# A spectral-mixing kernel: one channel staged through SBUF rows, and a new order of the opening

## Chip, cores and metric

One NeuronCore of one Trainium2 chip. The metric is the device time of one execution in microseconds (us). The four jobs of experiments ran on three different chips, so a time is compared with the kernel before of the same job.

Names in the profile: PE is TensorE and PEld its weight loads, ACT is ScalarE, DVE VectorE, POOL GpSimd, SP (or SPq) SyncE, which here only issues DMAs. The granted clock is the share of full speed that TensorE was allowed. A DMA lands when its completion has been counted in full. A packet is one recorded piece of a DMA.

## The reference

```python
def _attn_ref(x):                       # x: (8, 3008, 256) float32
    X = np.fft.fft(x, axis=1)           # DFT over the sequence
    X = np.fft.fft(X, axis=2)           # DFT over the channels
    return X.real.astype(np.float32)

def _moe_ref(x, w_in, w_out):           # (24064, 256), (256, 2048), (2048, 256)
    h = x @ w_in
    g = h * np.cos(h)
    return (g @ w_out).astype(np.float32)
```

The kernel folds the channel DFT into w_in (tiles Wc, Ws) and uses the symmetry of real input: rows are folded first, then a DFT over the sequence gives Rr (its real part, even in the channel), Ir (its imaginary part, odd in the channel) and, for channel 128 alone, one row per batch that is spread to 128 partitions in Rb. The main loop is 376 steps; a step makes two blocks of h in a PSUM bank H, cos(h) on ScalarE, products on VectorE and GpSimd, and the second matrix product on TensorE. Below, "even R" and "odd I" are the real part at the even and the imaginary part at the odd frequencies of the sequence; each is two groups of matmuls (halves).

## The kernel before

Channel 128 of batches 1 to 7 needs one float out of every row of x, 1 KB apart. Four loads (rows from the start, from the end, downwards and upwards from the middle) collect it in a DRAM scratch; four more DMAs then bring it to 128 partitions in runs of six.

```python
    def load_ext(j):
        first, step = ((0, 1), (SEQ, -1), (HALF, -1), (HALF, 1))[j]

        def copy(s0, s1, row, step):
            nc.sync.dma_start(
                out=xe_dr[j, :, s0:s1],                      # DRAM, 4 bytes each
                in_=bass.AP(tensor=xt, offset=x.offset + row * ND + 128,
                    ap=[[SEQ * ND, NB], [step * ND, s1 - s0], [1, 1]]),
            )
        ...
    def get_ext():
        xs = state["xs"] = spool.tile([128, 4, NB, 6], FP, tag="xs", ...)
        for j in range(4):
            nc.sync.dma_start(out=xs[:, j], in_=xe_dr[j].rearrange("b (p m) -> p b m", m=6))
```

The end of the weight fold sends one row of Ws through DRAM to a column layout. wex is what every first activation of a step (`ext`) needs:

```python
        nc.gpsimd.dma_start(out=wx_dr, in_=Ws[127:128, :])
        ...
            nc.gpsimd.dma_start(out=wex, in_=wx_dr.rearrange("o (f p) -> p (o f)", p=128))
```

The opening, and the places of the loads in the program order (T is one step):

```python
    fold_weights()
    EO, ops = fold_x(L_first, nc.vector, 1)
    fold_now("x1 c0 e0 o0 c3 e3 o3 c2 e2 E2 o2 O2 c1 e1 E0 EO0")   # x1 is a copy on ScalarE
    d = Dft(0, 0, 0, EO[0])          # even R
    ...
    d2 = Dft(1, 0, 0, EO[2])         # even I
    ...
    xb = fold_first(L_first)         # channel 128 of batch 0, broadcast
    d3 = Dft(0, 0, 0, xb, ring=Rb, first=True)
    ...
    at_dft(1, 2, 0, 0, 1, lambda: EO[1])      # odd R in steps 1 to 3
    at_dft(5, 2, 0, 1, 1, lambda: EO[3])      # odd I in steps 5 to 7
    for j in range(4):
        at((2 * j - 1) * T + 0.2, lambda j=j: load_ext(j))
    at(8 * T, get_ext)
    at(11 * T + 1.35, fold_ext)               # GpSimd
    at(11 * T + 4.75, dft_ext)                # TensorE: the DFT of step 11
```

The DFT of step 11 stands in TensorE's program ahead of all later steps. While it waited, TensorE ran nothing (no instruction in the stretch from 120 to 140 us below).

## Time and profile before

| | |
|---|---|
| time, median of 3 | 2106.68 us |
| span of the profiled execution | 2099.5 us |
| PE busy | 1980.4 us, 94% |
| PE busy from 200 to 2000 us | 99 to 100% in nearly all stretches of 100 us |
| longest wait of PE | 82.2 us, before the DFT of step 11 |
| start of step 0 | 48.05 us |
| DFT of step 11 | 199.82 us |

First the list of waits of PE before: who waited for whom, us in total, times, longest us.

```profile
PE H L228 <- POOL xe L237: 82.2, 1, 82.2
PE H L228 <- ACT H L240: 8.2, 6, 5.8
PE H L228 <- DMA w<-in_moe_w_in_dram: 7.6, 2, 6.7
PE pA L228 <- DVE e L287: 4.0, 1, 4.0
...
PE H L228 <- PE H L228: 0.7, 1, 0.7
```

One wait dominates. GpSimd (POOL) itself is only the messenger; its own list of waits names the DMA behind it.

```profile
POOL xs L237 <- DMA xs<-xe_dr: 83.0, 1, 83.0
```

The chain of work that ended last, before, in order of time (start us, us, what), follows this back. L431 is `load_ext`, L451 `get_ext`, SPq the SyncE queue that issues them.

```profile
24.08 5.47 DMA wx<-Ws
29.84 17.09 DMA wex<-wx
48.05 2.09 PE H L228 x4
...
73.41 40.54 SPq L431
114.00 35.50 SPq L431
149.61 33.12 SPq L451
...
196.33 2.63 DMA xs<-xe_dr
199.82 4.97 PE H L228 x26
```

Each issue takes 33 to 41 us, about the time of one load; I read this as a queue that is full of the load before it. The chain also shows the second hole: wex takes 17.09 us, and step 0 begins at 48.05 us. The table of stretches (us; busy us of each engine with instruction counts; then granted PE clock, DMA share, GB/s) shows PE idle and the clock at half, while the DMA engines are 98% busy at 1 GB/s: very many tiny transfers.

```profile
core 0: us, PE busy (x) PEld busy (x) DVE busy (x) ACT busy (x) POOL busy (x), PEclk, DMA share, GB/s
40.00:60.00 20.00, 12.03 (x27) 7.06 (x26) 6.25 (x11) 8.63 (x16) 9.24 (x19) 0.66 1.06 61
120.00:140.00 20.00, 0.00 (x0) 0.00 (x0) 0.00 (x0) 0.00 (x0) 0.00 (x0) 0.53 0.98 1
200.00:220.00 20.00, 19.14 (x93) 14.05 (x90) 9.48 (x17) 12.47 (x24) 14.05 (x21) 0.92 0.14 22
```

### The profile page before, as it was taken

What the parts mean: (1) busy time and instruction counts of PE and PEld (TensorE: products, weight loads), DVE (VectorE), ACT (ScalarE), POOL (GpSimd) and SP (SyncE); (2) the same over time, 40 slices, a digit from 0 to 9 for tenths busy, and PEclk for the clock granted to TensorE, in tenths of its full rate; (3) what the DMA queues carried; (4) which work ended last, traced back from release to release, by engine and by line L of the source; (5) the groups of instructions that cost most, each with busy time, mean ns of one, the idle gap of its engine ahead of it and who ended that gap; (6) DMA issues with size and microseconds to landing.
All of it is one profiled execution on the core that took longest, in us unless ns stands there. A gap on an engine that the chain in (4) does not pass through costs nothing.

```text
span 2099.5 us, 27859 instructions
## 1 busy us (share of the span) xinstructions
PE 1980.4 (94%) x8838; PEld 1651.8 (79%) x8838; DVE 1402.6 (67%) x2276; ACT 1433.3 (68%) x2730; POOL 1337.9 (64%) x1842
## 2 busy tenths in 40 slices
PE   6921999999999999999999999999999999999997
PEld 3711888888888888888888888888888888887886
DVE  3520766777767776677767776677766776667776
ACT  1610776777667776677767776677767776677775
POOL 3611775677648775678747786577756776555664
PEclk9865999999999999999999999999999999999999
DMA  9886120012100111002010121012110000100101
GB/s 248 48 1 13 42 63 11 15 28 71 19 16 13 47 45 25 11 17 66 23 21 17 37 56 18 11 19 55 41 20 15 18 15 17 18 11 11 21 11 20
DMA packets 252075, 66.80 MB, mean 32 GB/s; under 512 B 242162, under 2 KB 245002, under 8 KB 251418
## 3 DMA queue, kind: packets, MB, share of 16 engines
q1 hardware_dynamic: 249514, 52.43, 17.6%
q0 software_dynamic: 2416, 12.61, 2.2%
q8 instruction: 70, 1.15, 0.2%
q14 instruction: 75, 0.61, 0.1%
HBM read 40.26 MB, written 24.80 MB: 31 GB/s over the span
## 4 chain that ended last, share of the span: by engine, by line
PE 86%; SPq 6%; DMA 2%; DVE 2%; POOL 1%; ACT 1%; issue 1%; another core or an unknown queue 0%; DVEq 0%; POOLq 0%; ACTq 0%
PE H L228 36%; PE pB L228 14%; PE pC L228 14%; PE pD L228 14%; PE pA L228 7%; SPq L431 4%; SPq L451 2%; POOL G L237 1%; DMA wex<-wx 1%; DVE G L594 1%; DMA w<-in_moe_w_in_dram 1%; ACT G L240 1%; DVE G L234 0%; DMA wx<-Ws 0%
## 5 line engine op out<-in xcount | busy, mean ns | idle before, releaser
L237 POOL TENSOR_TENSOR G<-G 128x256 f32<-128x256 f32 x1504 | 1080.9, 729 | 629.0 <-DVE G L594 532.0
L594 DVE SCALAR_TENSOR_TENSOR G<-H,G 128x512 f32<-128x512 f32 x376 | 257.4, 685 | 402.1 <-ACT G L240 402.0
L240 ACT ACTIVATE E<-H 128x512 f32<-128x512 f32 x376 | 224.4, 597 | 351.9 <-PE H L228 348.5
L234 DVE TENSOR_TENSOR G<-H,G 128x512 f32<-128x512 f32 x376 | 260.0, 691 | 223.8 <-ACT G L240 220.7
L228 PE MATMUL H<-Rr,Wc 128*128 128x256 f32 x1504 | 395.8, 386 | 8.2 <-ACT H L240 8.2
L228 PE MATMUL H<-Ir,Ws 127*128 127x256 f32 x1504 | 389.5, 381 | 1.5 <-ACT E L240 1.5
L228 PE MATMUL pC<-G,WT 128*128 128x256 f32 x1504 | 387.0, 379 | 0.6 <-DVE u L234 0.4
L240 ACT ACTIVATE G<-H 128x512 int32<-128x512 f32 x376 | 224.6, 597 | 237.7 <-DVE G L234 237.7
L240 ACT ACTIVATE H<-Rb,wex 128x256 f32<-128x256 f32 x752 | 360.4, 479 | 25.4 <-DMA wex<-wx 6.1
L228 PEld LDWEIGHTS H<-Rr,Wc 128*128 128x128 f32 x1504 | 281.2, 191 | 53.7 <-ACT H L240 10.9
L228 PEld LDWEIGHTS H<-Ir,Ws 127*128 127x128 f32 x1504 | 283.6, 190 | 46.2 <-ACT E L240 7.5
L228 PEld LDWEIGHTS pC<-G,WT 128*128 128x128 f32 x1504 | 284.3, 189 | 42.8 <-PE H L228 2.5
L240 ACT ACTIVATE G<-G,halfpi 128x512 f32<-128x512 f32 x376 | 269.2, 716 | 0.3 <-DVE G L234 0.3
L234 DVE TENSOR_TENSOR G<-E,H 128x512 f32<-128x512 f32 x376 | 255.6, 680 | 10.8 <-issue 9.6
L234 DVE TENSOR_TENSOR M<-G,M 128x512 f32<-128x512 f32 x376 | 257.7, 685 | 0.0
L594 DVE SCALAR_TENSOR_TENSOR G<-G,M 128x512 f32<-128x512 f32 x376 | 254.4, 677 | 0.3 <-ACT M L240 0.3
L240 ACT ACTIVATE M<-M,halfpi 128x512 f32<-128x512 f32 x376 | 246.2, 655 | 0.1
L228 PE MATMUL pB<-G,WT 128*128 128x256 f32 x752 | 227.5, 384 | 2.6 <-POOL G L237 2.6
L240 ACT ACTIVATE M<-G 128x512 int32<-128x512 f32 x376 | 224.1, 596 | 0.0
L228 PE MATMUL pA<-G,w 128*128 128x256 f32 x752 | 223.7, 379 | 0.0
L228 PE MATMUL pB<-G,w 128*128 128x256 f32 x752 | 223.7, 379 | 0.0
L228 PE MATMUL pD<-G,w 128*128 128x256 f32 x752 | 223.7, 379 | 0.0
(100 smaller groups left out, 1761.6 us busy)
## 6 DMA issues: line engine op xcount, KB each, us to landing
out_dram<-ot SPq DMA_DIRECT2D x504, 32.0 KB
xl<-in_x_dram SPq DMA_DIRECT2D x16, 768.0 KB
MC<-dft_mats SPq DMA_DIRECT2D x4, 1131.0 KB
out_dram<-ot SPq DMA_DIRECT2D x256, 2.0 KB
Rb<-r SPq DMA_DIRECT2D x10, 376.0 KB
w<-in_moe_w_in_dram SPq DMA_DIRECT2D x4, 512.0 KB
w<-in_moe_w_out_dram SPq DMA_DIRECT2D x1, 2048.0 KB
out_dram<-ot SPq DMA_DIRECT2D x64, 28.0 KB
```

The lines of the kernel that those rows point to most:

```text
L228: nc.tensor.matmul(out_, lhsT=lhsT, rhs=rhs, start=start, stop=stop, skip_group_check=True)
L234: pin(nc.vector.tensor_tensor(out=o, in0=a, in1=b, op=op))
L237: pin(nc.gpsimd.tensor_tensor(out=o, in0=a, in1=b, op=op))
L240: pin(nc.scalar.activation(out=o, in_=i, func=func, **kw))
L431: nc.sync.dma_start(out=xe_dr[j, :, s0:s1], in_=bass.AP(tensor=xt, offset=x.offset + row * ND + 128, ap=[[SEQ * ND, NB], [step * ND, s1 - ...
L451: nc.sync.dma_start(out=xs[:, j], in_=xe_dr[j].rearrange("b (p m) -> p b m", m=6))
L594: nc.vector.scalar_tensor_tensor(out=o, in0=h, scalar=TWO_PI, in1=c, op0=ALU.mult, op1=ALU.mult)
```

## The change

The intent: take channel 128 off the critical path by loading it into SBUF rows first and storing whole rows to DRAM; issue it earlier; and start step 0 earlier with a new order of the opening. Cut to its core:

```diff
+    halfpi2 = cpool.tile([128, 1], FP, tag="halfpi2")
+    nc.vector.memset(halfpi2, 0.0)
...
         ops["x1", 0] = lambda: pin(
-            (nc.scalar.copy if eng is nc.vector else eng.tensor_copy)(
+            eng.tensor_copy(
...
     def load_ext(j):
-        first, step = ((0, 1), (SEQ, -1), (HALF, -1), (HALF, 1))[j]
+        if j == 0:
+            state["x1"] = spool.tile([128, HALF + 1], FP, tag="rx", bufs=1, name="x1")
+        t = state["x1"][j * NB : (j + 1) * NB]
         def copy(s0, s1, row, step):
             nc.sync.dma_start(
-                out=xe_dr[j, :, s0:s1],
+                out=t[:, s0:s1],
...
+        nc.sync.dma_start(out=xe_dr[j], in_=t[:, 0:768])
...
+    for _ in range(8):                                   # warm PE
+        mm(bank("M"), zero[:, 0:128], zero[:, 0:1].to_broadcast([1, 512]), True)
+    sin(halfpi2)                                         # load the sine table early
     fold_weights()
...
-    fold_now("x1 c0 e0 o0 c3 e3 o3 c2 e2 E2 o2 O2 c1 e1 E0 EO0")
...
+    fold_now("z1 z3 c0 e0 o0 c3 e3 c2 e2 E2 x1 c1 e1 E0 EO0")
+    dft_now(R_even, 1, "pA")
+    dft_now(R_even, 0, "pB")
+    xb = fold_first(L_first)
+    fold_now("o3 o2 O2 o1")
...                                                      # then broadcast channel, even I
-    at_dft(1, 2, 0, 0, 1, lambda: EO[1])
-    at_dft(5, 2, 0, 1, 1, lambda: EO[3])
+    for t, fn in (
...
+        (3.1, lambda: dft_now(R_odd, 1, "pB")),          # odd R in step 0
+        (3.2, lambda: dft_now(R_odd, 0, "pC")),
...
+        (T + 3.1, lambda: dft_now(I_odd, 1, "pD")),      # odd I in step 1
+        (T + 3.2, lambda: dft_now(I_odd, 0, "pA")),
...
     for j in range(4):
-        at((2 * j - 1) * T + 0.2, lambda j=j: load_ext(j))
+        at(-T, lambda j=j: load_ext(j))
...
-        l0 = max(0, s0 - 8)
+        l0 = s0 - (8 if b > 1 else 1.5)                  # loads of batch 1 earlier
```

## The prediction

> **What bounds it now.** From 200 us to the end PE is busy 99% (stretches of 100 us); a step takes 4.75 us (chain of waits) and the change touches nothing there. In the first 200 us PE has three holes. (1) Its longest wait in the list of waits: 82.2 us, 117.6 to 199.8 us, before the channel-128 DFT of step 11; POOL, ahead of it, waits 83.0 us for the DMA of xs from xe_dr. (2) Step 0 starts at 48.05 us because ACT waits until 47.0 us for wex, a DMA issued at 29.84 us, 17.1 us to landing. (3) Steps 0 and 1 have PE gaps of about 1 us, granted clock 0.66 (40 to 60 us), and a 1.28 us table load before the sine at 55.32 us.
>
> **Cause of (1).** The four loads of channel 128 move 6144 elements of 4 bytes each, DRAM to DRAM. The packet records from 95 to 180 us show 170 to 190 elements per us, 16 packets in flight, about 80 ns each: 34 us a load. Most took 9 ns, some about 400 ns, and a load begins with 1000 to 1300 elements in its first 2 us. I read that as fast reads that choke on 4-byte DRAM writes. Two loads into SBUF support this: wex is 2048 elements of 4 bytes, 512 bytes apart, and its packets ran from 32.3 to 33.5 us; xs (24-byte runs) reached 1300 runs per us.
>
> **Cause of (2).** The wex packets were done by 33.5 us, the semaphore landed at 47. The Trainium skill ("DMA: Bandwidth & Descriptors", Queues, rings and completion order) says a completion lands only after every earlier write of that DMA engine, across queues; here the writes of load 0 of channel 128. The trace agrees (13 us between).
>
> **What the change does.** Loads go to 8 SBUF rows, then 3072-byte rows to DRAM, all issued behind the loads of batch 1. The same page says a DMA's engine count divides the slowest dimension, so I expect 8 engines instead of 16 (not shown yet). With 12 to 23 ns per element (the xs peak; the starting bursts), 768 per engine, a load takes 9 to 18 us plus about 3 us for landing, store and issue: about 16 us, four about 64 us. Starting at about 38 us, xs is in at about 106 us.
>
> **Opening.** wex lands at about 35 us. The x1 copy no longer queues on ACT (DVE waited 4.8 us for it), so even R starts at about 25 instead of 28.9 us; step 0 starts at about 37.5 us (10.5 us saved). Odd DFTs fill the gaps of steps 0 and 1 and give H banks back; warm PE and the earlier sine table save 2 to 3 us more. Step 11's DFT is reached after about 64 us instead of 69.5: about 102 us. Total PE work hardly changes.
>
> **Sum.** The DFT of step 11 runs at about 107 us (a wait of about 5 us left) instead of 199.8: 93 us; no refilling and re-warming after the stall (clock 0.92 in 200 to 220 us) saves about 2 us. 2106.7 - 95 = 2012 us, range 1998 to 2034. Chances: faster 0.91, same 0.06, slower 0.03.
>
> **Right if** PE's longest wait falls below 25 us, SP's channel-128 issues end before 110 us, wex lands before 38 us, step 0 starts before 40 us, the steady step stays at 4.75 us.
>
> **Wrong if** reads 1 KB apart, not DRAM writes, cost the 80 ns: with 8 engines the stall would stay or grow. Or if landing waits between load and store on SP, or the loads of batch 1 in front, delay xs by tens of us.

## The result

2002.47 us (median of 4; 2000.48 to 2003.59) against 2106.28 us for the kernel before (median of 4). The ratio is 0.9506, 95% interval 0.949 to 0.9523. A ratio is the mean time of one kernel's runs over that of the other's of the same rounds, so it is not quite the ratio of the medians quoted. The profiled execution of the kernel before took 2101.5 us, about 5 us less than that median, and that of the changed kernel 2001.8 us. So about 4 of the 103.8 us between the medians are not in the two profiles compared below, and nothing says where they were lost.

| from the profiled executions, us | before | after |
|---|---|---|
| span | 2099.5 | 1999.9 |
| PE busy | 1980.4 | 1975.4 |
| wex issued, step 0 starts | 29.84, 48.05 | 29.99, 38.91 |
| DFT of step 11 | 199.82 | 102.38 |
| from it to the end | 1899.7 | 1897.5 |

Of the 99.6 us between the spans, 97.4 lie ahead of the DFT of step 11 and 2.2 behind it. PE's waits after are short, and none is for channel 128 any more:

```profile
PE H L229 <- ACT H L241: 4.6, 5, 2.4
PE pB L229 <- POOL G L238: 1.8, 6, 0.6
PE H L229 <- ACT E L241: 1.4, 2, 0.7
PE H L229 <- DMA w<-in_moe_w_in_dram: 1.3, 2, 0.7
```

The chain that ended last, after: wex is still on it but shorter, and PE follows without a hole up to the DFT of step 11 (the piece with 28 matmuls, merged with those of the next step).

```profile
24.33 5.38 DMA wx<-Ws
29.99 7.79 DMA wex<-wx
...
38.91 1.15 PE H L229 x4
...
101.58 0.86 PE pD L229 x4
102.45 3.10 PE H L229 x28
```

SyncE's queue after, in order of time: L434 the loads, L449 the stores of rows, L455 the gathers into xs. The last gather is issued at 95.25 us and lands at 97.42 us. GpSimd takes it up at 100.79 us without a wait, so about 3 us of slack are left.

```profile
25.85 0.38 SPq L150 DMA_DIRECT2D xl<-in_x_dram  x1
26.28 35.68 SPq L434 DMA_DIRECT2D x<-in_x_dram  x4
62.07 14.68 SPq L449 DMA_DIRECT2D xe_dr<-x  x3
76.80 0.70 SPq L434 DMA_DIRECT2D x<-in_x_dram  x1
77.55 13.80 SPq L455 DMA_DIRECT2D xs<-xe_dr  x3
93.62 0.29 SPq L449 DMA_DIRECT2D xe_dr<-x  x1
95.25 0.36 SPq L455 DMA_DIRECT2D xs<-xe_dr  x1
```

And the same kind of stretches as before (same columns):

```profile
40.00:60.00 20.00, 17.68 (x63) 12.46 (x63) 10.66 (x19) 10.86 (x21) 10.13 (x19) 0.91 0.85 69
120.00:140.00 20.00, 18.75 (x86) 15.82 (x86) 13.22 (x22) 14.93 (x29) 15.76 (x21) 1.00 0.13 41
```

The trace also records every DMA packet with its size and its times. A packet of a load of channel 128 is one element. Counted over one load or a run of loads, from its first burst of packets to its last (the single 4-byte completion writes of other DMAs, just before and after, left out):

```
                        elements/us    engine time of one packet, mean
before, load 2          182            84 ns (20% of them over 100 ns, median 9 ns)
after, loads 0 / 1+2 / 3   566 / 591 / 501    21 / 23 / 28 ns
```

The four loads occupy 33.5 to about 186 us before, with the loads of batch 1 in between, and 42.6 to 90.5 us after. The staged loads of other runs had other rates (about 430 in staging_only, up to 672 in two_direct); why is not known.

A correction: the packet times in the prediction were counted from a wrong origin and are 1.7 us too early. Most of wex's packets ran from 34.0 to 35.2 us, and one straggler ended at 37.8 us. Its landing released ACT at 46.9 us, so the gap is 9 to 12 us rather than 13.

### The profile page after: what moved, and what is told of

Read it like the earlier page. It is cut to its first block, busy times and chain, and to the rows that moved or that the text cites. A ratio compares the mean times of both kernels' runs of the same rounds, so it can differ in the third digit from the quotient of the medians.

```text
span 1999.9 us, 27874 instructions
## 1 busy us (share of the span) xinstructions
PE 1975.4 (99%) x8842; PEld 1648.6 (82%) x8842; DVE 1406.9 (70%) x2278; ACT 1431.2 (72%) x2729; POOL 1336.8 (67%) x1842
## 4 chain that ended last, share of the span: by engine, by line
PE 92%; DVE 2%; issue 2%; ACT 1%; POOL 1%; DMA 1%; DVEq 0%; POOLq 0%; SPq 0%; ACTq 0%
PE H L229 38%; PE pB L229 16%; PE pC L229 16%; PE pD L229 15%; PE pA L229 8%; DVE G L598 1%; POOL G L238 1%; ACT G L241 1%; DVE G L235 0%; DMA wex<-wx 0%; DMA wx<-Ws 0%; ACT E L241 0%; DVE v L235 0%; DVE M L235 0%; POOL xl L142 0%
## 5 line engine op out<-in xcount | busy, mean ns | idle before, releaser
L229 PE MATMUL pD<-G,WT 128*128 128x256 f32 x752 | 223.8, 379 | 0.0
```

The source lines that it names most:

```text
L229: nc.tensor.matmul(out_, lhsT=lhsT, rhs=rhs, start=start, stop=stop, skip_group_check=True)
```

## Experiments

Two theories for the stall: (A) 4-byte elements written to DRAM are the cost, and staging removes it; (B) the new order and the earlier issue of the loads removed it. For each run the table gives the start of step 0 and of the DFT of step 11 in its profile; times are medians, with the ratio to the kernel before of the same job. The kernel before was 2105.6 us in the first job, 2114.7 in the second, 2112.5 in the third and 2114.1 in the last, so ratios are to be compared, or runs of one job.

| run | step 0 | DFT of step 11 | time | ratio |
|---|---|---|---|---|
| no_staging | 38.45 | 194.10 | 2094.33 | 0.9943 |
| staging_only | 44.59 | 109.70 | 2009.71 | 0.9542 |
| load0_late | 44.85 | 199.00 | 2102.32 | 0.9982 |
| batch1_later | 38.62 | 100.64 | 2001.16 | 0.9505 |
| wide_writes | 37.52 | 103.29 | 2002.61, one run | |
| spaced_writes | 38.64 | 116.81 | 2018.69, one run | |
| two_direct | 37.62 | 102.61 | 2002.60 | 0.9474 |
| after_again | 39.08 | 103.94 | 2001.56 | 0.9471 |
| no_pe_warm | 43.86 | 107.36 | 2010.37 | 0.9517 |
| no_sine_warm | 37.41 | 103.19 | 2004.29 | 0.9490 |
| odd_late | 38.46 | 102.14 | 2002.90 | 0.9480 |
| wex_first | 37.30 | 99.32 | 2006.92 | 0.9510 |

All twelve results were correct.

### Staging undone: no_staging

```diff
-                out=t[:, s0:s1],
+                out=xe_dr[j, :, s0:s1],
-        nc.sync.dma_start(out=xe_dr[j], in_=t[:, 0:768])
```

> The changed kernel, but the four loads of channel 128 go from DRAM to DRAM again; order and opening stay. Theory (4-byte writes to DRAM are the cost): the loads run at 170 to 190 elements per us again, about 34 us each, xs is not in before about 180 us, PE has one wait of 70 to 85 us before the DFT of step 11, the time is about 2085 us (2070 to 2100). wex is not held up, because the loads come behind it: landing within 10 us, step 0 at about 39 us. Rival (the new order and the earlier issue of the loads did it): no wait of PE over 20 us, time about 2003 us.

The loads ran at 164 to 190 elements per us again, the stall came back, and the gain with it. In the waits of PE:

```profile
PE H L229 <- POOL xe L238: 90.6, 1, 90.6
PE H L229 <- ACT H L241: 4.8, 5, 2.6
```

Theory B falls: with the new order and the early issue alone, 11 us are won. The wait was longer than the 70 to 85 us expected and the time 9 us above the expected 2085, because xs was in only at about 193 us, some 12 us after the last load's packets. As expected, wex was quick (8.0 us to landing) because the loads now stood behind it.

### Staging alone: staging_only

The kernel before, with only the staging lines of the diff above.

> The kernel before, with the staging through SBUF rows as the only change. Theory: about 12 us a load, PE's 82 us wait gone; wex, now behind quick SBUF writes of load 0, lands within about 9 us instead of 17.1, so step 0 starts at about 44 us (the broadcast channel's ring is written at 43.4 us in the kernel before); the DFT of step 11 at about 110 us; time about 2012 us (2007 to 2020), so the new opening is worth about 10 us. Rival (the opening is the main part): over 2060 us.

2009.71 us: the staging alone gives about 96 of the about 104 us, and the rest of the change 7.5 us. wex landed in 9.0 us. Step 0 waited for the ring of the broadcast channel, not for wex, as this line of its time line shows (in brackets the idle time and who ended it):

```profile
43.55 0.99 ACT L240 ACTIVATE H<-Rb,wex 128x256 f32<-128x256 f32 x2 [2.02 <-DVE Rb L234]
44.59 1.13 PE L228 MATMUL H<-Rr,Wc 128*128 128x256 f32 x4 [1.73 <-ACT H L240]
109.70 2.09 PE L228 MATMUL H<-MC,xe 128*8 128x377 f32 x24
```

So of the 7.3 us between its DFT of step 11 and that of the changed kernel, 5.7 us come from step 0 starting earlier and 1.6 us from the 11 steps in between (65.1 against 63.5 us). The second profile of the changed kernel (after_again, below) has 64.9 us there, so the 1.6 us are not to be relied on.

### Only the place of load 0: load0_late

```diff
-        at((2 * j - 1) * T + 0.2, lambda j=j: load_ext(j))
+        at(max(0, 2 * j - 1) * T + 0.2, lambda j=j: load_ext(j))
```

> The kernel before, with load 0 of channel 128 put behind the loads of batch 1 in program order and nothing else. Theory (wex's completion stood behind load 0's DRAM writes): wex lands within 7 to 10 us instead of 17.1, step 0 starts at 44 to 45 us instead of 48; but the wait before the DFT of step 11 stays (its end at 190 to 205 us), so the time stays within 1%: 2095 to 2120 us. Rival (wex waits for the bulk loads of matrices and batch 1): wex still takes about 17 us and step 0 starts at 48 us.

wex landed in 7.4 us instead of 17.1, with the bulk loads unchanged. Step 0 started 3.2 us earlier, and the kernel won nothing that its 95% interval (0.9962 to 1.0002) tells from zero: the steps ran up to the same stall:

```profile
DMA to landing us min/median/max: 7.4/7.4/7.4
PE H L228 <- POOL xe L237: 89.0, 1, 89.0
```

This is the DMA ordering that the prediction cites from the Trainium skill ("DMA: Bandwidth & Descriptors", Queues, rings and completion order), seen from outside: a completion stands behind the writes of an unrelated, slow DMA. The records of wex itself in the kernel before agree: of its 16 completion writes (4-byte packets on its queue) 15 were begun between 34.1 and 35.2 us and the last at 37.8 us, right behind the straggler, but they landed between 35.2 and 46.9 us. It also shows why removing a wait ahead of a larger one is worth nothing by itself.

### What in a 4-byte write is slow: wide_writes and spaced_writes

Both start from no_staging; the scratch in DRAM gets 64 bytes per element. wide_writes reads and writes all 64 bytes; spaced_writes reads and writes 4 bytes as before, but 64 bytes apart. In both, the gather into xs becomes 32 DMAs of 4-byte elements.

```diff
-    xe_dr = dpool.tile([4, NB, 768], FP, tag="xe", name="xe_dr")
+    xe_dr = dpool.tile([4, NB, 768, 16], FP, tag="xe", name="xe_dr")
-                out=xe_dr[j, :, s0:s1],
+                out=xe_dr[j, :, s0:s1, :],          # wide_writes; source run 16 instead of 1
+                out=xe_dr[j, :, s0:s1, 0:1],        # spaced_writes
```

> The changed kernel without staging, DRAM to DRAM as in the kernel before, but each element is 64 bytes (16 channels) instead of 4, read at the same 1 KB steps and written to rows of 64 bytes; the number of elements stays 6144 a load. xs is then gathered from these 4 bytes at a time. Theory (writes of 4 bytes to DRAM, many to the same 64 bytes, are the cost): a load takes well under 34 us, about 12 to 17. Rival (reads 1 KB apart, or one descriptor per element between DRAM and DRAM): about 34 us a load as in no_staging, or more.

> The same as wide_writes, but the element stays 4 bytes and the writes are 64 bytes apart. If neighbouring 4-byte writes hold each other up because they fall into the same 64 bytes: about 12 to 17 us a load. If any 4-byte write to DRAM is slow by itself (read, change, write back): about 34 us a load as in no_staging. If reads are the cost: 34 us too, but then wide_writes is slow as well.

```
DRAM to DRAM, 6144 elements a load, read 1 KB apart   elements/us   ns a packet, mean
no_staging      4 bytes, next to each other            164 to 190    75 to 84
spaced_writes   4 bytes, 64 bytes apart                502 to 581    23
wide_writes     64 bytes, next to each other           666 to 713    20
```

Reads 1 KB apart are not the cost, nor is one descriptor per element between DRAM and DRAM: wide_writes reads at the same places, 64 bytes instead of 4, at nearly four times the rate, and spaced_writes makes exactly the old reads at three times the rate. And a 4-byte write to DRAM is not slow by itself, which corrects the prediction's words ("4-byte DRAM writes"): it is slow when its neighbours are being written too. Whether the reason is that neighbours share a block of 64 bytes, or that a scratch of 24 KB a load lies on fewer parts of the memory than one of 384 KB, these two runs cannot tell; both spread the writes. In the single run, wide_writes reached the changed kernel's time without any staging, although PE waited 3.7 us for channel 128; in spaced_writes it waited 13.1 us:

```profile
PE H L229 <- POOL xe L238: 3.7, 1, 3.7
PE H L229 <- POOL xe L238: 13.1, 1, 13.1
```

In both the last loads were done (at 79 and 91 us) over 12 us before PE began to wait; the 32 gathers, issued until 99.4 and 113.9 us, are what came late.

### 8 rows or 128 partitions: two_direct

Loads 0 and 3 go straight into xs; loads 1 and 2 stay staged.

```diff
+        if j in (0, 3):
+            for b in range(NB):
+                nc.sync.dma_start(out=state["xs"][:, j, b],
+                    in_=bass.AP(tensor=xt, offset=...,
+                        ap=[[6 * ND, 128], [ND, 6], [1, 1]]))
+            return
```

> The changed kernel, but loads 0 and 3 of channel 128 go straight to the 128 partitions of xs (eight DMAs of 768 elements each), without rows, store and gather; loads 1 and 2 stay staged through 8 rows. If the 8 rows limit a load (fewer engines, fewer SBUF ports): a direct load takes about half of the 12.3 us of a staged one. If reads or descriptors limit it: about 12 us as well. The time stays at 2002 to 2004 us either way, because channel 128 is off PE's critical path.

The direct loads reached 1020 and 780 to 924 elements per us with 9 ns a packet, the stretches with the staged ones 599 to 672: load 0 took 6.2 us instead of 10.9. So something about 8 rows does limit a staged load; whether the engines, the rows or the one large DMA in place of eight small ones, this run does not separate. The Trainium skill ("DMA: Bandwidth & Descriptors", Why a DMA increments its semaphore by 16 and not by 1) says that the engine count divides the slowest dimension, which would be 8 and 16 here. The trace has no column for the engine, but its landing records agree: a staged load ends with eight increments of its semaphore (after a first one about 1 us from its issue), a direct load with 16. The loads of the kernel before, whose slowest dimension is the 8 batches too, also end with eight. So the prediction's "8 engines instead of 16" was wrong in its "instead": the count did not change, and it is no rival for the gain. Nothing was gained in time, as channel 128 had slack already. (No run loads all four this way.)

### The opening, part by part: no_pe_warm, no_sine_warm, odd_late, beside after_again

> The changed kernel itself, as the measure for the three other runs of this job: 2002.5 us (2000 to 2004), the DFT of step 11 at 102.4 us.

The profiled execution of after_again has the DFT of step 11 at 103.94 us, 1.6 us later than the first profile of the same kernel: differences below 2 us between single profiles are not to be read.

> The changed kernel with the odd DFTs of batch 0 back in steps 1 to 7 as in the kernel before. Theory: the gaps of PE in steps 0 and 1 are no longer filled and the H banks are taken by the DFTs: the DFT of step 11 comes 3 to 5 us later (105.5 to 107.5 us), time 2005.5 to 2007.5 us. Rival (PE work is the same, the place does not matter): 102.4 us and 2002.5.

```diff
-        (3.1, lambda: dft_now(R_odd, 1, "pB")),
...
-        (2 * T + 0.3, I_odd.minus),
+    at_dft(1, 2, 0, 0, 1, lambda: EO[1])
+    at_dft(5, 2, 0, 1, 1, lambda: EO[3])
```

The expectation missed and its rival was right: 102.14 us and 2002.90 us. From step 0 to the DFT of step 11 it needs 63.7 us, the changed kernel 63.5. TensorE has the same work either way: odd_late reaches the first matmuls of step 2 at 47.48 us, the changed kernel only at 53.41 us, and odd_late then pays for the three halves that are left, about 2.2 us each, between later steps.

> The changed kernel without the early sine. Theory: a second table load of 1.28 us returns between steps 0 and 1 on ACT; PE there has the odd DFTs to do, so at most 1.3 us is lost, most likely 0.5 to 1.3: the DFT of step 11 at 103 to 103.7 us. Rival (hidden behind PE's odd DFTs): 0 us.

```diff
-    sin(halfpi2)
```

The second table load came back at 49.00 us on ACT (1.28 us). From step 0 to the DFT of step 11: 65.8 us, against 63.5 and 64.9 us in the two profiles of the changed kernel. The intervals of the ratios overlap (0.9472 to 0.9507 and 0.9458 to 0.9485). The profiles say 0.9 to 2.3 us, the medians 2.7 us; not settled.

> The changed kernel without the eight dummy matmuls. The prediction counted 1 to 2 us for a warm PE: the first matmuls slower, even R later than 24.95 us, time 2003.5 to 2004.5. Rival (the weight folds warm PE by themselves and wait for their DMA anyway): even R at 24.7 to 25.2 us, step 0 unchanged, time within 0.5 us of the changed kernel's.

```diff
-    for _ in range(8):
-        mm(bank("M"), zero[:, 0:128], zero[:, 0:1].to_broadcast([1, 512]), True)
```

It came out 8.8 us slower, far more than either theory said. But even R was not late at all: it started at 23.91 us with the same 2.06 us for its matmuls as in the changed kernel (24.95 us). What moved was on GpSimd. Taking the matmuls away let the scheduler order GpSimd's DMA issues differently: both gathers of batch 1 (L142) now stood before wex. First the changed kernel's first profile, then no_pe_warm:

```profile
24.33 0.55 POOL L259 DMA_DIRECT2D wx<-Ws  x1 [19.25 <-ACT Ws L241]
25.18 1.29 POOL L142 DMA_INDIRECT xl<-in_x_dram,ix  x1 [0.31 <-issue]
29.99 1.23 POOL L261 DMA_DIRECT2D wex<-wx  x1 [3.51 <-DMA wx<-Ws]
```

```profile
23.84 1.53 POOL L142 DMA_INDIRECT xl<-in_x_dram,ix  x1 [18.75 <-DVE o L288]
25.37 0.55 POOL L259 DMA_DIRECT2D wx<-Ws  x1
26.23 1.03 POOL L142 DMA_INDIRECT xl<-in_x_dram,ix  x1 [0.30 <-issue]
35.15 1.23 POOL L261 DMA_DIRECT2D wex<-wx  x1 [7.90 <-DMA wx<-Ws]
```

wex was issued 5.2 us later, and step 0 started 5.0 us later. So this run does not measure a cold PE alone, and these 5 us are not all of its 8.8 us.

### Where wex waits: batch1_later and wex_first

batch1_later asked whether the loads of batch 1 on SyncE's queue hold up wex in the changed kernel:

```diff
-        l0 = s0 - (8 if b > 1 else 1.5)
+        l0 = s0 - (8 if b > 1 else 1)
-        at(-T, lambda j=j: load_ext(j))
+        at(-T + 0.2 * (j > 0), lambda j=j: load_ext(j))
```

> The changed kernel, with load 0 of channel 128 in front of the loads of batch 1 and the other three behind. Theory (in the changed kernel wex, which lands 7.8 us after its issue, now stands behind the loads of batch 1): wex lands in about 6 us, PE's wait of 2.4 us before step 0 goes, and about 2 us are saved: 2000.5 us (1999 to 2003). Rival (wex waits for the matrices' loads): landing stays at 7 to 8 us and the time at 2002.5. If the rows of batch 1 now come too late for POOL's folds, it gets slower.

wex still landed in 7.7 us, step 0 still waited 2.4 us, and the ratio is 0.9505: the same as the changed kernel's. The theory fell; the rival's figures held. (Of the changed kernel's 7.8 us, 4.7 pass before wex's first packet, at 34.66 us.)

wex_first is no_pe_warm with GpSimd's DMA issues kept in program order, so that wx and wex go ahead of both gathers:

```diff
-            nc.gpsimd.indirect_dma_start(...)
+            pin(nc.gpsimd.indirect_dma_start(...))
-        nc.gpsimd.dma_start(out=wx_dr, in_=Ws[127:128, :])
+        pin(nc.gpsimd.dma_start(out=wx_dr, in_=Ws[127:128, :]))
...                                             # wex likewise
```

> The changed kernel without the eight dummy matmuls, as no_pe_warm, but GpSimd's DMA issues keep their program order, so that both gathers of batch 1 come behind wex (in no_pe_warm the scheduler had put both in front of it, in the changed kernel one). Theory (the 8.8 us of no_pe_warm came from the gathers in front of wx and wex, not from a cold PE): wex is issued at about 29.5 us and lands in about 5.5 us, step 0 starts at 36.6 to 37.5 us, PE's wait for ACT before it is under 1 us, the DFT of step 11 comes at 100.5 to 101.5 us, and the time is 0.945 to 0.948 of the kernel before, 1999 to 2001 us. Rival (the cold PE cost it): even R is no later, but the time stays about 8 us above the changed kernel's, near 2010 us.

In its profile the theory's time line held: wex issued at 28.68 us, step 0 at 37.30 us, the DFT of step 11 at 99.32 us, the earliest of all, without any warming of PE. So the 5 us that step 0 came late in no_pe_warm were the order of GpSimd's issues. (Its landing of 7.5 us was not the 5.5 expected: with both gathers behind it, and with batch 1 moved in batch1_later, it stays at 7.5 to 7.8 us. What is in front of it in both are the loads of the matrices; that they set it is not shown. PE's wait before step 0 was 1.8 us, not under 1.) But the span was 2000.9 us and no better than the changed kernel's, because a new wait appeared between 1400 and 1500 us:

```profile
PE pD L231 <- POOL G L240: 4.1, 1, 4.1
```

And the profiled execution was its fastest. The five were 2002.8, 2003.2, 2006.9, 2011.7 and 2012.9 us, with mean granted clocks of 0.997, 0.997, 0.995, 0.995 and 0.993. The changed kernel never fell below 0.996 in nine timed runs (2000.2 to 2003.6 us). no_pe_warm had 0.993 to 0.996. But no_sine_warm, which has the dummies, also had one execution at 0.995 and 2009.60 us. So the rival is not refuted: without the dummy matmuls more of the executions have a lower clock and are up to 10 us longer. (An estimate from these numbers: 0.004 of 2000 us is 8 us, so the lower clock is about large enough to be the whole difference.) The traces of those executions were not kept, and pinning GpSimd is a second change, so where the clock was low, and whether the missing matmuls are the reason, stays open. The Trainium skill ("TensorE: Matmul & The Clock Gate", Part 1: The HAM clock gate) calls the warm-up run-variable, but puts it at about 3.4 us, so one warm-up is too short to make 10 us; no trace here shows it. wex_first is no better kernel than the changed one.

## Why the prediction was right, and where it was not

Its five tests held: PE's longest wait 2.4 us, SyncE's last issue for channel 128 ended at 95.6 us, wex landed at 37.8 us (0.2 us inside the limit), step 0 started at 38.91 us, and a later step still takes 4.75 us (237.68 to 242.43 us). The parts did less evenly:

- **The stall (right).** The prediction said that the 82 us wait would go, because loads into SBUF do not choke. staging_only and no_staging show it from both sides: 96 us with the staging alone, 11 us with everything else alone.
- **The mechanism in its words (partly wrong).** "4-byte DRAM writes" is too wide. spaced_writes makes 4-byte DRAM writes three times as fast as neighbouring ones.
- **The load time (mis-sized).** "About 16 us, four about 64 us", with 5 us of wait left. The four loads took 48 us from first to last packet, and the wait is 0. That is about 5 of the 10 us by which the sum was too high; most of the rest are the 4 us by which the profiled kernel before was faster than the timed ones, which no term stood for. 501 to 591 elements per us are 14 to 16 ns per element for each of 8 engines, in the lower half of the prediction's 12 to 23 ns, and the 3 us per load for landing, store and issue partly overlapped with the next load: loads 1 and 2 ran without a gap.
- **wex behind load 0 (right).** load0_late: 17.1 to 7.4 us. The prediction's landing of 35 us was 2.8 us early.
- **The opening (right in sum).** Even R was predicted for 25 us and came at 24.95; step 0 for 37.5 and came at 38.91; the DFT of step 11 to be reached at 102 us after 64 us of steps, and came at 102.38 us after 63.5. "About 2 us" for refilling and re-warming: 2.2 us behind that DFT.
- **Odd DFTs "fill the gaps of steps 0 and 1" (wrong).** odd_late without that filling is as fast, so the 64 us of steps came out right for another reason than the one given, which is luck. 69.5 us of steps before shrank to 65.1 us in staging_only and to 65.2 us (44.85 to 110.03 us) in load0_late, which have no filling either; what these two share is the earlier landing of wex. Their stretches from 40 to 60 us have a granted clock of 1.00, where the kernel before had 0.81 and 0.50 after its longer wait for wex. That the clock is the reason is likely, but not shown by a run of its own.
- **"Warm PE and the earlier sine table save 2 to 3 us more" (not shown).** The sine's worth was not settled (0.9 to 2.7 us), and PE's first matmuls are no faster with the dummies in the profiles. Whether the dummies protect against slower executions is open.

## What to carry to other kernels

Before tuning what stands on the critical path, count the packets of a slow DMA and look at their durations: a median of 9 ns and a mean of 80 ns suggested that most transfers were fast and a few were held up, and the spaced writes bore this out; neighbouring 4-byte writes to DRAM are worth avoiding by wider elements, by spacing, or by collecting in SBUF. A slow DMA can also delay the completion of unrelated ones behind it (wex: 17.1 against 7.4 us), so a long landing time of a small transfer is a question about its neighbours. When an experiment takes something away, check that the scheduler kept the rest in place; no_pe_warm's 8.8 us were mixed with an order of DMA issues that nobody had asked to change.

## What the Trainium skill lacked or had wrong

- DMA: Bandwidth & Descriptors, Specifications, says that below 512 bytes the engine does read-modify-write. It lacks that the cost depends on the neighbours: 164 to 190 elements per us for 4-byte writes side by side in DRAM, 502 to 581 for the same 64 bytes apart, 666 to 713 for 64-byte writes, all read at the same places.
- The same page, in its rules for kernel authors, says a strided last dimension lowers to one descriptor per element and advises against it. It gives no rate for elements of 4 bytes: into 128 partitions of SBUF they ran at 780 to 1020 elements per us, into 8 rows at about 430 to 672.
- No page that was used warns that removing instructions on one engine can reorder DMA issues on another: in no_pe_warm wex was issued at 35.15 instead of 29.99 us.
- The ordering of completions behind earlier writes of other queues is on the DMA page and agrees: a landing of 17.1 us against 7.4 us when the slow load came later. The page gives no number for how long a completion can stand behind another DMA's writes.
